# A recurrent attention and a two-layer FFN on one core: transposes by DMA of two chunks in one transfer, the first pair in halves by heads, and a new order of all steps

## The chip, the cores and the metric

The kernel runs on one core of one Trainium2 chip. A core has five engines with instruction streams of their own: TensorE (PE) multiplies matrices, VectorE (DVE), ScalarE (ACT) and GpSimd (POOL) work elementwise, and SyncE (SP) issues nearly all DMAs. The metric is the device time of one execution in microseconds (us); lower is better. Before the change three runs took 182.15, 182.19 and 182.31 us, median 182.19.

## The reference

Inputs `r`, `k`, `v`, `w` have the shape (4, 8, 768, 48): batch, heads, sequence, head dimension, in float32. For each batch and head a 48 x 48 state runs over the sequence, and the result goes through a feed-forward network (FFN) with a leaky relu:

```
for t in range(S):
    cur     = u * k_t  outer  v_t
    y_t     = r_t @ (state + cur)
    state   = w_t[:, None] * state + k_t outer v_t
x = y as (3072 tokens, 384)
out = max(0.01 h, h) @ w_out,   h = x @ w_in      # 384 -> 2048 -> 384
```

## The kernel before

**Chunks.** The sequence is cut into chunks of 128 positions, six for each of four batches, 24 in all. Inside a chunk the decays become a cumulative sum of logarithms, so that with r' = r exp(sum) and k' = k exp(-sum) the outputs are a masked product: scores = k' r'^T for all eight heads, times a triangular mask, times v, plus r' times the state that came in. The bonus with u is a term of its own (POOL products, a DVE reduction, a POOL product). Chunks 0 to 3 are done as two *pairs* (function `pair`: two chunks of one batch at once, with positions interleaved), and chunks 4 to 23 by `single`.

**Steps of a single chunk.** Four loads (L701, SP, 192 KB each) bring w, k, r, v into one "in" slot. ACT takes the logarithm (L711), PE the cumulative sum (L717, L720), DVE adds (L729), ACT makes the two exponentials (L743, L747), DVE the products r' and k' into an "rk" tile (L405). Then rk is transposed to rkT, either by PE (L416, evacuated by DVE L421 or ACT L423) or by one DMA transpose on SP's queue (L764): the set `RK_DMA` says which chunks go by DMA, 13 of them. PE makes the scores (L858), for one chunk or, where `MERGED` says so, for two chunks in one step. DVE masks them (L788), PE multiplies by v and by the state (L829, L824), DVE adds the bonus and writes y (L478). y is transposed into xT, by PE (L464) and a copy (L469, L471), or by a DMA transpose (L843) for the eight chunks in `Y_DMA`. The state goes on through L798 and L811 or L813, with POOL's L775.

**Steps of a pair.** One load brings both chunks of a tensor, 384 KB (L490). One logarithm (L502), three cumulative sums (L510), a total (L524), four exponentials of 384 columns (L543), four products (L405), four transposes by PE, scores in two steps (L624), four masks of 512 columns (L636), sums (L583), the state (L594, L601), intra (L649), inter (L656), bonus (L668), two copies to y (L678, L680), two transposes.

**FFN.** The list `blocks` groups the chunks into blocks of one or two. For each block an up step (L901) is six matmuls of 256 columns for a block of two, or twelve of 128 for a block of one, into one PSUM bank of 512 columns; ACT applies the leaky relu (L916); a down step (L928) is four matmuls of 384 columns. DVE or ACT copies a chunk's output (L939, L941) and SP stores it (L945). The FFN weights come in float32 and are cast to bf16 by ACT, DVE and POOL (L357 to L361), each into place from an "in" slot.

**What sets the order.** Nothing is scheduled on the chip: every engine runs its list from first to last, and waits where an input is not there. The class `Plan` makes the lists while the program is built. It holds steps with durations for each engine that could do them, priorities (chunk number times ten, the FFN from 1000 on), buffers from pools of fixed size, and a model of the DMA queue with a wire time for each kind of transfer. It steps through time and starts, on each free engine, the ready step of lowest priority number whose buffers are free. `RANK` shifts the priority of single steps, `FORCE` fixes the engine. Where the plan sees PE idle in the first 24 us, it adds filler matmuls on zeros (L970).

**Queues.** All loads, stores and transposes are on SP's one queue, in the order of the list, each issue waiting for its own buffers and for the transfer eight places before it.

Of the kernel before, what the change touches and what calls it, by code (L numbers as in the profile page):

```python
# [8 lines left out]
F32 = mybir.dt.float32  # L9
BF16 = mybir.dt.bfloat16  # L10
# [5 lines left out]
class Buf:  # L16


    def __init__(self, pool, kind=None):
        self.pool, self.kind, self.users, self.t, self.free_at = pool, kind or pool, [], None, 0.0  # L20


class Plan:
# [18 lines left out]
    def order(self, pools):  # L42
# [10 lines left out]
        remain = {k: len(b.users) for k, b in bufs.items()}  # L53
        free_tiles = {p: [(0.0, k) for k in range(len(t))] for p, t in pools.items()}
# [18 lines left out]
        while events:  # L73
# [13 lines left out]
            for e in self.ENGINES:  # L87
# [3 lines left out]
                while ready[e]:  # L91
                    pri, i = heapq.heappop(ready[e])
                    if self.start[i] is not None:
                        continue
                    want, ok = {}, True
                    for b in self.steps[i][5]:
                        if b.t is None:
                            want[b.pool] = want.get(b.pool, 0) + 1
                            if in_use.get(b.kind, 0) >= self.limits.get(b.kind, 99):
                                ok = False  # L100
                    for p, k in want.items():
                        if sum(f <= now + 1e-9 for f, _ in free_tiles[p]) < k:
                            ok = False
# [10 lines left out]
                for b in takes:  # L114
                    if b.t is None:
                        slots = free_tiles[b.pool]
                        s = min(slots)
                        slots.remove(s)
                        b.slot = s[1]
                        b.t = pools[b.pool][s[1]]  # L120
                        in_use[b.kind] = in_use.get(b.kind, 0) + 1
# [9 lines left out]
                else:  # L131
# [5 lines left out]
                    self.done[i] = dma_free + lat + (self.late if now > 20 else 0.0)  # L137
                heapq.heappush(events, (free[e], 1, e, -1))
# [5 lines left out]
                for b in {id(b): b for b in (*reads, *takes)}.values():  # L144
                    b.free_at = max(b.free_at, self.done[i])
                    remain[id(b)] -= sum(u == i for u in b.users)
                    if remain[id(b)] == 0:
                        free_tiles[b.pool].append((b.free_at, b.slot))
                        heapq.heappush(events, (b.free_at, 2, "*", b.kind))
# [6 lines left out]
BOTH = (1.5, 64, 1.45, 0.2)  # L156
WEIGHT = (2.08, 24, 2.6, 0.2)
# [4 lines left out]
RANK = {0: 15.37, 1: 14.4, 2: 3.33, 3: 23.03, 4: 38.76, 5: 12.01, 6: -26.8, 7: -21.87, 8: -21.96, 9: -19.05,  # L162
# [16 lines left out]
FORCE = {23: "DVE", 26: "DVE", 29: "ACT", 30: "DVE", 46: "ACT", 58: "ACT", 61: "ACT", 79: "ACT", 85: "DVE",  # L179
    112: "DVE", 114: "ACT", 117: "DVE", 119: "ACT", 121: "ACT", 123: "DVE", 125: "POOL", 127: "ACT", 128:  # L180
    "POOL", 134: "POOL", 137: "DVE", 139: "POOL", 142: "ACT", 143: "POOL"}
# [3 lines left out]
def kernel(  # L185
# [37 lines left out]
    blocks = [2, 1, 1, 1, 1, 2, 2, 2, 2, 2, 1, 1, 2, 2, 2]  # L223
# [17 lines left out]

    trev = pool.tile([128, 128], BF16, name="trev")
# [12 lines left out]
    xT = pool.tile([128, KT, NCH * L], BF16, name="xT")  # L255

    make("in", 10, [128, 1536], F32)
    make("lw", 3, [128, H, 64], BF16)
    make("lw2", 1, [128, 2, H, 64], BF16)
    make("ci", 2, [128, H, D], F32)  # L260
    make("rk", 5, [128, 2, H, 64], BF16)
    make("rkT", 4, [128, 2 * NP, 128], BF16)
    make("rkT2", 2, [128, 2 * NP, 256], BF16)
    make("vb", 6, [128, H, D], BF16)
    make("ru", 2, [128, H, D], F32)
    make("dg", 3, [128, H], F32)
    make("vs", 4, [128, H, D], F32)
    make("m", 3, [128, 2, NP, 128], BF16)
    make("a", 3, [128, NP, 2], F32)
    make("s", 6, [128, NP, 2, D], F32)  # L270
    make("sb", 4, [128, NP, 2, D], BF16)
    make("y", 4, [128, H, D], BF16)
    make("g", 3, [128, NJ, max(blocks) * L], BF16)
    make("o", 5, [128, DM], F32)
    make("ps", 8, [128, 512], F32, psum)

    with tc.manual_schedule():
# [41 lines left out]
        plan = Plan({"hp": 2, "op": 2, "cp": 1, "ek": 1, "yy": 2, "warm": 1, "warm2": 1}, SLACK_FROM, SLACK, LATE)  # L319
# [87 lines left out]
        def transposes(P0, rk, kind, s_d, rkTb, out_of, pri_k=0):  # L407
# [6 lines left out]
            def tpose(e):  # L414
                for g in range(NP):
# [3 lines left out]
            def evac(e):  # L419
                if e == "DVE":  # L420
                    nc.vector.tensor_copy(out=out_of(), in_=view()[:, 0:NP, :])  # L421
                else:
                    nc.scalar.copy(out=out_of(), in_=view()[:, 0:NP, :])  # L423

            s_tr = step({"PE": 0.23}, tpose, P0, deps=[s_d], reads=[rk], takes=[tr])
            return step({"DVE": 0.42, "ACT": 0.59}, evac, P0, deps=[s_tr], reads=[tr], takes=[rkTb])
# [48 lines left out]
        def add_bonus(P0, y, yp, vs, s_y, s_vs):  # L475
            return step(
                {"DVE": 0.55},
                lambda e: nc.vector.tensor_tensor(out=y.t[:], in0=heads(yp.t), in1=vs.t[:], op=ALU.add),  # L478
                P0 + 1, deps=[s_y, s_vs], reads=[yp, vs], takes=[y])
# [3 lines left out]
        def pair(n):  # L483
            P0 = n * 10
            b = seq[n][0]
            slots = [Buf("in"), Buf("in")]
            lds = {}
            for name, src, si, off in (("w", w, 0, 0), ("k", k, 0, 1), ("r", r, 1, 0), ("v", v, 1, 1)):
                def load(e, src=src, si=si, off=off):
                    nc.sync.dma_start(  # L490
                        out=slots[si].t[:, off * 768 : (off + 1) * 768].rearrange("p (h f) -> p h f", h=H),
                        in_=src[b, :, 0 : 2 * L, :].rearrange("h (p j) d -> p h (j d)", j=2))
                lds[name] = [step({"SP": 0.65}, load, P0 + len(lds) * 0.1, takes=[slots[si]], wire=BOTH)]

            def view(si, off, j):
                return lambda: slots[si].t[:, off * 768 : (off + 1) * 768].rearrange(
                    "p (h j d) -> p h j d", h=H, j=2)[:, :, j, :]

            lw = Buf("lw2")
            s_ln = lns[n] = step(  # L500
                {"ACT": 0.85},
                lambda e: nc.scalar.activation(  # L502
                    out=lw.t[:, :, :, 0:D].rearrange("p j h d -> p h j d"),
                    in_=slots[0].t[:, 0:768].rearrange("p (h j d) -> p h j d", h=H, j=2), func=AF.Ln),
                P0, deps=lds["w"], reads=[slots[0]], takes=[lw])

            def cum(bank, mats):
                def go(e):
                    for j in range(2):
                        nc.tensor.matmul(  # L510
                            heads(bank.t), lhsT=mats[j][:], rhs=lw.t[:, j, :, 0:D], start=(j == 0), stop=(j == 1),
                            skip_group_check=True)
                return step({"PE": 0.33 if n else 0.55}, go, P0, deps=[s_ln], reads=[lw], takes=[bank])

            c1, c0, cg, e0 = (Buf("ps", "cp2") for _ in range(4))
            s_c1 = cum(c1, (tstr2, tinc2))
            s_c0 = cum(c0, (tinc2, tinc2))
            s_cg = cum(cg, (tstr2, tstr2))
            firsts[n] = s_c1
# [485 lines left out]
```

## Time and profile before

| | |
|---|---|
| median of three runs | 182.19 us |
| the profiled execution | 181.38 us |
| its span, first to last instruction | 179.6 us |
| mean granted PE clock | 0.996 |
| PE busy | 171.6 us (96%) |
| DVE, ACT, POOL busy | 115.0, 115.3, 102.5 us |
| DMA moved | 34.43 MB in 116571 packets |
| first FFN matmul | 19.00 us |
| last score step of the attention | 156.84 us |
| matmuls end, last copy begins | 176.0 us |
| DMA transposes rkT: count, median to landing | 13, 3.9 us |
| DMA transposes xT: count, median to landing | 8, 3.7 us |

The page is a sum over one execution. "Busy" of PE counts each matmul from start to end, and matmuls overlap in the array, so 96% is not 96% of peak; what a matmul costs the stream is read from the distance of the starts in the timeline. Idle time stands behind a group with the work that ended it. The chain of waits is followed back from the last instruction.

### The profile page before, as it was taken

How to read it: one execution, taken by the hardware profiler on the slowest of the kernel's cores; microseconds unless marked ns; L12 is line 12 of the kernel's file. 1: busy time of each engine (PE TensorE's matmuls, PEld its weight loads, DVE VectorE, ACT ScalarE, POOL GpSimd, SP SyncE). 2: the span in 40 equal slices, each digit the busy share in tenths (PEclk: the TensorE clock that was granted, in tenths of full speed). 3: DMA queues.
4: the chain of work that ended last, by engine and by line, in shares of the span. 5: the costliest groups of instructions: out<-in, count | busy, mean ns of one | idle time of the engine just before them, and what ended most of it. 6: DMA issues, size and time to landing. Idle time of an engine off the chain costs nothing.

```text
span 179.6 us, 5197 instructions
## 1 busy us (share of the span) xinstructions
PE 171.6 (96%) x2036; PEld 129.8 (72%) x2037; DVE 115.0 (64%) x231; ACT 115.3 (64%) x253; POOL 102.5 (57%) x138
## 2 busy tenths in 40 slices
PE   7798999999999999999999999999999999999991
PEld 2466888867778788877788767787788786787850
DVE  7699764289789898559677558397468297241102
ACT  2678968855867788884489774485486664652610
POOL 5999632574897686877469854667165665100000
PEclk9999999999999999999999999999999999999998
DMA  5999999998999999999999989999899996600112
GB/s 141 261 283 316 370 376 364 187 199 199 231 191 224 180 229 134 184 213 173 185 181 223 212 179 223 153 215 175 152 254 170 220 163 134 167 9 19 47 44 88
DMA packets 116571, 34.43 MB, mean 192 GB/s; under 512 B 109121, under 2 KB 115778, under 8 KB 116546
## 3 DMA queue, kind: packets, MB, share of 16 engines
q1 hardware_dynamic: 116544, 34.09, 95.8%
q8 instruction: 16, 0.26, 0.7%
q14 instruction: 9, 0.07, 0.1%
q10 hardware_dynamic: 2, 0.00, 0.0%
HBM read 25.17 MB, written 4.72 MB: 166 GB/s over the span
## 4 chain that ended last, share of the span: by engine, by line
PE 77%; DMA 11%; DVE 4%; ACT 2%; issue 2%; SPq 1%; POOL 0%; DVEq 0%; ACTq 0%
PE ps L901 35%; PE ps L928 28%; DMA in<-in_r_dram 3%; DMA in<-in_v_dram 3%; DMA in<-in_w_dram 2%; PE ps L858 2%; DMA xT<-y 2%; PE ps L829 2%; PE ps L717 2%; PE ps L824 2%; PE ps L416 2%; DVE rk L405 2%; PE ps L798 1%; PE ps L464 1%; DVE m L636 1%
## 5 line engine op out<-in xcount | busy, mean ns | idle before, releaser
L901 PE MATMUL ps<-xT,w_in_b 128*128 128x256 bf16 (+1 forms) x720 | 73.3, 251 | 0.4 <-ACT xT L471 0.2
L928 PE MATMUL ps<-w_out_b,g 128*128 128x384 bf16 x384 | 73.4, 326 | 0.0
L916 ACT ACTIVATE g<-ps 128x512 bf16<-128x512 f32 x96 | 56.8, 597 | 25.4 <-PE ps L901 23.2
L901 PEld LDWEIGHTS <-w_in_b 128*128 128x128 bf16 x720 | 57.8, 98 | 9.9 <-issue 0.7
L928 PEld LDWEIGHTS <-g 128*128 128x128 bf16 x384 | 35.2, 98 | 17.3
L405 DVE TENSOR_TENSOR rk<-in,ps 128x384 bf16<-128x384 f32 x46 | 24.5, 548 | 9.9 <-ACT ps L743 6.5
L435 POOL TENSOR_TENSOR ru<-in,ub 128x384 f32<-128x384 f32 x24 | 23.9, 1001 | 9.6 <-DMA in<-in_k_dram 7.6
L788 DVE TENSOR_TENSOR m<-ps,maskb 128x512 bf16<-128x512 f32 x40 | 25.1, 683 | 5.3 <-PE ps L858 5.3
L439 POOL TENSOR_TENSOR ru<-ru,in 128x384 f32<-128x384 f32 x24 | 24.6, 1027 | 3.0 <-DMA in<-in_r_dram 2.4
L775 POOL TENSOR_TENSOR sb<-s,a 128x384 bf16<-128x384 f32 x18 | 15.0, 831 | 16.8 <-ACT a L738 16.8
L447 POOL TENSOR_TENSOR vs<-in,dg 128x384 f32<-128x384 f32 x20 | 16.6, 830 | 9.1 <-DVE dg L443 8.4
L729 DVE TENSOR_TENSOR ci<-ps,lw 128x384 f32<-128x384 f32 x20 | 11.1, 555 | 9.7 <-PE ps L720 4.5
L939 DVE COPY o<-ps 128x384 f32<-128x384 f32 x10 | 5.6, 555 | 15.6 <-PE ps L928 15.4
L443 DVE TENSOR_REDUCE dg<-ru 128x8 f32<-128x384 f32 x24 | 12.9, 544 | 2.1 <-POOL ru L439 2.1
L478 DVE TENSOR_TENSOR y<-ps,vs 128x384 bf16<-128x384 f32 x20 | 11.1, 553 | 3.2 <-PE ps L829 2.6
L455 POOL CAST vb<-in 128x384 bf16<-128x384 f32 x24 | 12.0, 504 | 1.5 <-DMA in<-in_v_dram 1.4
L711 ACT ACTIVATE lw<-in 128x384 bf16<-128x384 f32 x20 | 10.4, 522 | 2.9 <-DMA in<-in_w_dram 2.9
L743 ACT ACTIVATE ps<-ps 128x384 f32<-128x384 f32 x20 | 9.6, 481 | 4.1 <-DVE ci L729 3.6
L738 ACT ACTIVATE a<-ps 64x4 f32<-64x4 f32 x36 | 6.0, 167 | 7.7 <-DVE ci L729 5.1
L813 DVE TENSOR_TENSOR s<-ps,sb 128x384 f32<-128x384 f32 x14 | 7.7, 552 | 3.8 <-PE ps L798 2.7
L747 ACT ACTIVATE ps<-ci 128x384 f32<-128x384 f32 x20 | 9.8, 491 | 0.0
L941 ACT COPY o<-ps 128x384 f32<-128x384 f32 x14 | 6.7, 479 | 4.2 <-PE ps L928 4.0
(90 smaller groups left out, 176.2 us busy)
## 6 DMA issues: line engine op xcount, KB each, us to landing
out_dram<-o SPq DMA_DIRECT2D x24, 192.0 KB, 3.7
in<-in_w_dram SPq DMA_DIRECT2D x20, 192.0 KB, 4.2
in<-in_k_dram SPq DMA_DIRECT2D x20, 192.0 KB, 4.2
in<-in_r_dram SPq DMA_DIRECT2D x20, 192.0 KB, 4.0
in<-in_v_dram SPq DMA_DIRECT2D x20, 192.0 KB, 4.0
in<-in_moe_w_out_dram SPq DMA_DIRECT2D x4, 768.0 KB, 12.1
in<-in_moe_w_in_dram SPq DMA_DIRECT2D x4, 384.0 KB, 6.8
in<-in_moe_w_in_dram SPq DMA_DIRECT2D x2, 768.0 KB, 9.0
```

Source lines behind the costliest of these rows:

```text
L405: (nc.gpsimd if e == "POOL" else nc.vector).tensor_tensor(out=o, in0=x, in1=i, op=ALU.mult)
L435: lambda e: nc.gpsimd.tensor_tensor(out=ru.t[:], in0=kv(), in1=ubv, op=ALU.mult),
L439: lambda e: nc.gpsimd.tensor_tensor(out=ru.t[:], in0=ru.t[:], in1=rv(), op=ALU.mult),
L443: lambda e: nc.vector.tensor_reduce(out=dg.t[:], in_=ru.t[:], axis=AX.X, op=ALU.add),
L447: lambda e: nc.gpsimd.tensor_tensor(out=vs.t[:], in0=vv(), in1=dg.t[:].unsqueeze(2).to_broadcast([128, H, D]), op=ALU.mult),
L455: {"POOL": 0.56}, lambda e: nc.gpsimd.tensor_copy(out=vb.t[:], in_=vv()),
L478: lambda e: nc.vector.tensor_tensor(out=y.t[:], in0=heads(yp.t), in1=vs.t[:], op=ALU.add),
L775: lambda e: nc.gpsimd.tensor_tensor(out=sb.t[:].rearrange("p g a d -> p (g a) d"), in0=s_in.t[:].rearrange("p g a d -> p (g a) d"), in1=a_ ...
L788: lambda e, par=par: nc.vector.tensor_tensor(out=m.t[:, par, :, :], in0=sc[par].t[:].rearrange("p (g t) -> p g t", g=NP), in1=maskb[:].uns ...
L901: nc.tensor.matmul(hp.t[:, a * N : (a + 1) * N], lhsT=w_in_b[:, t, (j + a) * 128 : (j + a + 1) * 128], rhs=xT[:, t, c0 : c0 + N], start=(a ...
L916: lambda e, hp=hp, g=g, j=j, J=J, N=N: nc.scalar.activation(out=g.t[:, j : j + J, 0:N], in_=hp.t[:, 0 : J * N].rearrange("p (a n) -> p a n ...
L928: nc.tensor.matmul(op.t[:, 0:DM], lhsT=g.t[:, j, off : off + 128], rhs=w_out_b[:, j, :], start=(j == 0), stop=(j == NJ - 1))
```

## The change

1. **Merged transposes.** Where two chunks' scores are merged, their rk tiles are now two neighbouring slots of one tile, and one DMA transpose (128 x 2048 elements) fills two neighbouring rkT slots. It is issued after both chunks' r' and k'. In the same way a pair's two y tiles go in one transfer (128 x 768) into two neighbouring chunks of xT, whose layout becomes chunk by chunk. There are 6 merged and 1 single rk transpose (13 single before) and 4 merged and 2 single for y (8 single before). Chunks 22 and 23 become a merged pair.
2. **The first pair in halves.** For the pair at chunk 0, loads of w, k and r, the logarithm, the cumulative sums, exponentials, products, transposes, scores and masks are done for four heads at a time. In both pairs intra becomes two steps or four by parity and half, and the order of the products that are added into y is free.
3. **Buffers.** "in" 10 to 7, lw 3 to 2, rk stays 5 and rkT becomes 5 in place of 4 + 2 wide ones, vb 6 to 10, ru 2 to 3, vs 4 to 3, m 3 to 5, s 6 to 5, y 4 to 3, g 3 to 2, o 5 to 24. Limits on PSUM banks: up results ("hp") 2 to 4, cumulative sums and one exponential 1 to 2, attention outputs 2 to 4.
4. **The plan.** It also keeps PE from starting on a bank that another engine still uses; 0.4 us are added to every DMA after 20 us (0 before), the slack of 0.2 us a step goes; `RANK` has a number for nearly every step in place of 144, `FORCE` is new, and `blocks` has 14 entries, four of them of one chunk, in place of 15 with six.

By the lists, PE has 25 fillers in place of 40, 12 score steps for the singles in place of 13, and 42 transposes of y in place of 48; the 88 of rk stay. SP's list has the first store behind 38 loads of the singles, where it was behind nine. The copy of ub (L399) goes from DVE to ACT.

```diff
-    RK_DMA = {6, 11, 12, 14, 15, 16, 17, 18, 19, 20, 21, 22, 23}
-    Y_DMA = {8, 10, 16, 17, 20, 21, 22, 23}
-    MERGED = {6, 10, 12, 14, 16, 18, 20}
-    LEAD = 4
-    AHEAD = 4
-    SLACK_FROM = 50
-    SLACK = 0.2
-    LATE = 0.0
+    RK_DMA = {9, 12, 13, 14, 16, 17, 18, 19, 20, 22}
+    Y_DMA = {13, 14, 15, 17, 18, 19, 20, 22}
+    MERGED = {6, 10, 12, 14, 16, 18, 20, 22}
+    PARTS = {0: [(0, NP // 2), (NP // 2, NP)]}
+    HALVES = "wkr"
+    LIMITS = {"hp": 4, "op": 2, "cp": 2, "ek": 2, "yy": 4, "warm": 1, "warm2": 1}
+    LEAD = 6
+    AHEAD = 7
+    SLACK_FROM = 45
+    SLACK = 0.0
+    LATE = 0.4
...
-    blocks = [2, 1, 1, 1, 1, 2, 2, 2, 2, 2, 1, 1, 2, 2, 2]
+    blocks = [2, 2, 1, 1, 2, 1, 2, 2, 1, 2, 2, 2, 2, 2]
...
+    def make2(name, count, shape, dtype):
+        t = pool.tile([shape[0], count, *shape[1:]], dtype, name=name)
+        pools[name] = [t[:, i] for i in range(count)]
+        pools[name + " wide"] = [t[:, i : i + 2] for i in range(count - 1)]
...
-    xT = pool.tile([128, KT, NCH * L], BF16, name="xT")
+    xT = pool.tile([128, NCH, KT, L], BF16, name="xT")
...
+            parts = PARTS.get(n, [(0, NP)])
...
+                cuts = parts if name in HALVES else [(0, NP)]
+                for x, (g0, g1) in enumerate(cuts):
...
+            for x, (g0, g1) in enumerate(parts):
+                P = x, g0, g1
+                wide = (g1 - g0) / NP
+                s_k0 = exp(c1, e0, -1.0, [s_c1[x]], [c1], [e0], *P)
...
         def run(ns):
-            works = [single(n) for n in ns]
+            two, P1 = None, ns[-1] * 10
+            if len(ns) == 2:
+                rk2, rkT2 = (Buf("rk", wide=2), Buf("rkT", wide=2)) if ns[0] in RK_DMA else (None, None)
+                two = [rk2, rkT2, Buf("y", wide=2) if ns[0] in Y_DMA else None, [], [], []]
+            works = [single(n, two, x) for x, n in enumerate(ns)]
             asked = [next(x) for x in works]
+            if two and two[0]:
+                two[4].append(step(
+                    {"SP": 1.3},
+                    lambda e: nc.sync.dma_start_transpose(
+                        out=rkT2.t.rearrange("p x g t -> p (x g) t"), in_=rk2.t.rearrange("p x a h d -> p (x a h d)")),
+                    P1, deps=two[3], reads=[rk2], takes=[rkT2], wire=TRK2))
...
+            if two and two[2]:
+                s_x = step(
+                    {"SP": 1.3},
+                    lambda e: nc.sync.dma_start_transpose(
+                        out=xT[:, ns[0] : ns[0] + 2].rearrange("p x g t -> p (x g) t"),
+                        in_=two[2].t.rearrange("p x h d -> p (x h d)")),
+                    P1 + 1, deps=two[5], reads=[two[2]], wire=TY2)
```

More of the change, by code (lines that the diff above doesn't have):

```diff
@@ L113, in order @@
                 engs, fn, pri, deps, reads, takes, wire = self.steps[i]
[L114 to L121, printed above, removed]
+                for b, k in given:
+                    gone = range(k, k + b.wide)
+                    free_tiles[b.pool] = [x for x in free_tiles[b.pool] if x[1] not in gone]
+                    b.slot = k
+                    b.t = pools[b.pool if b.wide == 1 else b.pool + " wide"][k]
+                    in_use[b.kind] = in_use.get(b.kind, 0) + 1
                 d = engs[e]
@@ L137, in order @@
                     self.done[i] = dma_free + lat + (self.late if now > 20 else 0.0)
+                for b in (*reads, *takes):
+                    if e == "PE":
+                        b.written = max(b.written, self.done[i])
+                    else:
+                        b.other = max(b.other, self.done[i])
                 heapq.heappush(events, (free[e], 1, e, -1))
@@ L156 @@
 BOTH = (1.5, 64, 1.45, 0.2)
+PART = (0.75, 32, 1.45, 0.2)
 WEIGHT = (2.08, 24, 2.6, 0.2)
@@ L414, in tpose @@
             def tpose(e):
-                for g in range(NP):
+                for g in range(g0, g1):
                     nc.tensor.transpose(
@@ L497, in view, with some, cum @@
                     "p (h j d) -> p h j d", h=H, j=2)[:, :, j, :]
+            def some(name, g0, g1):
+                return [*{x: 0 for x in lds[name][g0:g1]}]
             lw = Buf("lw2")
[L500 to L507, printed above, removed]
+            s_lns = [step(
+                {"ACT": 0.16 + 0.69 * (g1 - g0) / NP},
+                lambda e, h0=2 * g0, h1=2 * g1: nc.scalar.activation(
+                    out=lw.t[:, :, h0:h1, 0:D].rearrange("p j h d -> p h j d"),
+                    in_=slots[0].t[:, 0:768].rearrange("p (h j d) -> p h j d", h=H, j=2)[:, h0:h1, :, :], func=AF.Ln),
+                P0 + 0.5 * x, deps=some("w", g0, g1), reads=[slots[0]], takes=[lw]) for x, (g0, g1) in enumerate(parts)]
+            lns[n] = s_lns[0]
+            def cum(bank, mats, x, g0, g1):
                 def go(e):
@@ new lines, in pair, with summed, intra @@
+            yps, begun = [Buf("ps", "y2"), Buf("ps", "y2")], set()
+            def summed(x, out, **k):
+                nc.tensor.matmul(out, start=x not in begun, stop=True, skip_group_check=True, **k)
+                begun.add(x)
+            s_yi = []
+            for i, (g0, g1) in enumerate(parts):
+                for par in range(2):
+                    def intra(e, g0=g0, g1=g1, par=par):
+                        for h in range(2 * g0 + par, 2 * g1, 2):
+                            for js in range(2):
+                                for x in range(2):
+                                    q = slice(64 * x, 64 * x + 64)
+                                    summed(x, yps[x].t[:, h * D : (h + 1) * D], lhsT=ms[js].t[q, par, h // 2, :],
+                                           rhs=vbs[js].t[q, h, :])
+                    s_yi.append(step(
+                        {"PE": 0.35 * (g1 - g0) / NP}, intra, P0 + 1, deps=[s_ms[i, 0, par], s_ms[i, 1, par], *s_vbs],
+                        reads=[*ms, *vbs], takes=yps))
@@ L664, in add_vs @@
+            s_y1 = step(
+                {"PE": 0.19}, inter, P0 + 1, deps=[s_sb, *(s for x in s_T for s in x)], reads=[rkTb, sb], takes=yps)
             def add_vs(e):
```

314 lines of the change are left out of this document (177 added, 137 removed), and 149 rows, old and new, of the table RANK.

## The prediction

> **What bounds the kernel now.** I read the page's busy shares and slices first, then the table by stage, then the chain that ended last, then the TensorE (PE) timeline around each pause.
>
> ```profile
> span 179.6 us, 5197 instructions
> ...
> PE 171.6 (96%) x2036; PEld 129.8 (72%) x2037; DVE 115.0 (64%) x231; ACT 115.3 (64%) x253; POOL 102.5 (57%) x138
> ...
> PEclk9999999999999999999999999999999999999998
> ...
> 0.00:19.00 19.00, 15.41 (x225) 9.35 (x227) 15.51 (x43) 12.32 (x26) 15.82 (x31) 1.00 1.05 257
> ...
> 25.70:156.80 131.10, 130.58 (x1558) 101.30 (x1557) 90.18 (x173) 90.38 (x207) 82.58 (x101) 1.00 1.09 199
> ```
>
> PE is busy 130.58 of 131.10 us between 25.7 and 156.8 us. From 25.7 us on, the end is set by how much PE still has to stream, plus its few pauses. Before 19 us it is not PE: VectorE (DVE) is busy 15.51 of 19, and many PE instructions are fillers. The chain says so too:
>
> ```profile
> 1.93 5.64 DMA in<-in_r_dram
> 7.67 0.99 DVE rk L405
> ...
> 11.32 0.27 DVE m L636
> ...
> 13.59 0.68 DVE m L636
> ...
> 18.22 0.74 ACT xT L471 x2
> 19.00 1.47 PE ps L901 x12
> ```
>
> The first pair waits for r (7.67), then runs through DVE to its last mask multiply (13.59 + 0.68 = 14.27), through ScalarE (ACT) to xT, and the first FFN matmul starts at 19.00. So three things count: the opening, PE's sum afterwards, PE's pauses afterwards. Two of the pauses, and one that is no wait:
>
> ```profile
> 47.86 0.36 PE L829 MATMUL ps<-vb,m 128*128 128x48 bf16 x8
> 48.45 0.32 PE L717 MATMUL ps<-lw,trev 128*128 128x384 bf16 x1 [0.23 <-ACT lw L711]
> ...
> 54.15 0.62 PE L858 MATMUL ps<-rkT 48*128 48x128 bf16 x16
> 54.70 0.51 PE L901 MATMUL ps<-xT,w_in_b 128*128 128x128 bf16 x6
> ...
> 61.05 0.82 PE L928 MATMUL ps<-w_out_b,g 128*128 128x384 bf16 x4
> 62.08 0.70 PE L901 MATMUL ps<-xT,w_in_b 128*128 128x256 bf16 x5 [0.20 <-ACT xT L471]
> ```
>
> Starts, not durations, give PE's price, because matmuls overlap. Eight of L829 stream in 0.20, but 0.59 passes: 0.38 lost, waiting for a w load. Four of L928 take 0.65, but 1.03 passes: 0.37 lost, waiting for an xT copy. With four smaller ones (52.9, 60.6, 88.3, 116.9: 0.19, 0.10, 0.14, 0.07) the real waits after 25.7 us are 1.25. At 54.15 sixteen score matmuls occupy 0.55 where pairs of them stream in about 0.45, and the instruction ahead of them is held 0.10 too: each score step costs about 0.2 beyond its columns.
>
> **The change, part by part.** Prices by starts: up step of 256 columns (6 matmuls) 0.655, matmul of 128 columns 0.056, of 384 columns 0.1625.
>
> *PE's sum.* Two more y chunks are transposed by DMA (before 8, after 10: singles 13 and 17, pairs from 14, 18, 20, 22): 6 x 0.056 = -0.33. Four one-chunk FFN blocks in place of six: 96 matmuls of 128 columns become 48 of 256: 5.38 - 5.23 = -0.14. One more merged pair, so 12 score steps for 13: -0.22. Sum -0.7. The rk transposes by PE stay 88, and 13 chunks of rk go by DMA as before (six pairs and one single).
>
> *The opening, in halves.* DVE's price per column follows from two rows:
>
> ```profile
> L405 DVE TENSOR_TENSOR rk<-in,ps 128x384 bf16<-128x384 f32 x46 | 24.5, 548 | 9.9 <-ACT ps L743 6.5 <-ACT ps L747 2.4 <-ACT ps L543 0.8
> L788 DVE TENSOR_TENSOR m<-ps,maskb 128x512 bf16<-128x512 f32 x40 | 25.1, 683 | 5.3 <-PE ps L858 5.3
> ```
>
> That is 0.145 fixed and 0.00105 a column, so a half rk costs 0.35 and a half mask 0.41. By the new order: the halves of w let Ln end at about 5.1 (before 5.42). The copy of ub now stands on ACT ahead of the exponentials, until 5.65. Half exponentials (0.31) follow, and DVE starts at 6.3 (before 6.51). DVE then has rk 6 x 0.35 + 2 x 0.47 (those that read ci from SBUF are dearer, 792 against 548), three evacuations 0.7, two reductions 1.09, eight half masks 3.3: 8.1, plus about 0.4 of waiting for exponentials. Last mask at 14.8, against 14.27, and the second pair's first rk (0.54) is not yet done, as it was before. From there: two rk and sb (1.65), the inter matmuls (0.4), then in ACT's order two y copies, an rkT evacuation, two xT copies, and the cast of w_in that the first up step needs (0.49 x 2 + 0.62 + 0.49 x 2 + 0.85): 14.8 + 1.65 + 0.4 + 3.4 = 20.3 for the first up, against 19.00. The new order has fewer holes behind it: by 25.9 us both have done all of both pairs, and the old one 36 up matmuls of 256 columns and some of the next block, the new one 30. Behind by 6 x 0.109 + 0.2 = 0.85. I take +0.9. Bounds: -0.5, if the halves pull the chain forward by the 0.7 us that half a load takes and ACT's order costs nothing; +1.6, if the DVE work meets POOL as the 0.98 us rk at 7.67 did.
>
> A step more of scores in the first pair also costs PE its 0.2; DVE's lateness covers that, and without the cover it is +0.2. [...]
>
> *Merged transposes.* They move the same blocks of 128 columns, so no DMA work is saved, but SP issues 13 transposes for 21. Their issues take 1.2 to 1.9 us of SP each; SP waits for others most of the time, so the gain is 0. Landing:
>
> ```profile
> DMA to landing us min/median/max: 3.0/3.9/5.7
> ...
> DMA to landing us min/median/max: 2.3/3.7/4.9
> ```
>
> The first line is rkT (8 blocks), the second xT (3 blocks). Five more blocks cost 0.7 at the minimum, 0.14 each: a merged rk transfer lands 1.1 later, a merged y 0.4 later. Bounds: 0, and a second whole landing (3.9, 3.7). Both chunks must now be ready before the issue, and loads queued on SP behind it wait too. What hides it is PE work between a chunk's last input and its use, summed from the new order. For rk, from the pair's last cumulative sum to the scores: 10.6 us for 16/17, 12.3 to 17 for the others. The chain needs 0.3 + 0.55 + 1.0 + 1.1 + 0.5, then 5.7 + 1.1: 10.2. For y, from intra to the first up: 8.4 for 14/15, 6.4 for 18/19, 5.2 for 20/21, 4.55 for 22/23. Need 0.75 + 4.9 + 0.4 = 6.1 while loads run, 0.75 + 2.3 + 0.4 = 3.5 at the end. So 0, with little to spare at 16/17 and 18/19.
>
> *Buffers and order.* Ten input slots become seven, two g buffers for three, 24 o buffers for five. The last weights are issued after casts that free their slots, so I see DMA idle for 1.2 to 1.7 us near 21 us. In exchange the stores move behind: the w load that was late at 47.9 us was the fifteenth transfer after the weights, and is the twelfth; a load of 192 KB at the 199 GB/s of the stage table takes 1.0 us. That wait goes. Next late: xT of one-chunk blocks, where 0.8 to 1.05 us of PE work covers about 0.8; 0.1 to 0.2 each. I take 0.55 of waits after 25.7 us. Bounds 0.3 and 3.0 (six score steps each waiting as long as the worst before, and the three tight y).
>
> Sum: 0.9 - 0.7 - 1.25 + 0.55 = -0.5. The profiled execution took 181.38 (span 179.6, 1.8 around it), so it would become 180.9. That execution lies 0.8 under the median of the runs, so the forecast is 182.19 - 0.5 = **181.7**.
>
> **The rivals.**
> - *The opening loses more* (slower). Halves add nine fixed parts of about 0.145 on DVE (four rk, four masks, one evacuation). Against: DVE idled 0.61 before r. With the opening at +2.0: 2.0 - 0.7 - 1.25 + 0.55 = +0.6, 182.8. It decides for slower from an opening 1.8 behind. Chance 0.18.
> - *The transposed pair comes late*. At 18/19, 20/21 and 16/17 PE stands until the transfer lands. For it: PE runs its list in order, and landing reached 5.7. From 1.5 times the single landing on it shows; at the bound of a second landing 18/19, 20/21 and 16/17 lose 1.8, 2.9 and 1.7, about +5.5. Middle +2, 184.2. Chance 0.16.
> - *The halves do shorten the opening*: -0.5 - 0.7 - 1.25 + 0.55 = -1.9, 180.3. For it: r's wait of 0.61 goes. Chance 0.22.
> - *The clock falls*. Fillers fall from 40 matmuls to 25. PE's first matmuls of 512 columns take 0.427, the one at 5.08 takes 0.226, and the clock stays 1.00 over pauses of 0.8. Opening work at half speed for a stretch of 3.4 us: +1.7, 183.4. Chance 0.02. [...]
>
> **How the numbers follow.** The forecast's case, 181.1 to 182.2, has 0.4: 0.26 of it faster, 0.14 within 0.2% (0.36 us, about what a measurement of this kernel can tell). Faster: 0.26 + 0.22 = 0.48. Same: 0.14 + 0.04 from the edges of the slow cases = 0.18. Slower: 0.14 + 0.15 + 0.02 + 0.03 unnamed = 0.34. The range runs from the third rival to the middle of the second, 180.3 to 184.2.
>
> **What would show it.** Right: last half mask near 14.8 us, first up near 20.3, PE without a hole from 26 us on, no score step waiting for rkT, 1.1 us more to landing for merged rk. Wrong: first up before 19; PE idle at up steps behind a merged y; DMA holes between 40 and 110 us with PE waiting for lw; a PE clock under 1.00 before 20 us.

## The result and the profile after

The changed kernel took 183.95 us (median of five, 183.89 to 185.60), the kernel before beside it 182.19 (five, 181.34 to 183.07). The ratio is 1.0123, 95% interval 1.0074 to 1.0172: slower by 1.2%, where 0.3% faster was forecast. The ratios here and below are worked out from the fast runs of both kernels (those at most 1.5% above the fastest of the same kernel; here with a sixth run of 184.83), and not from the two medians, which alone would give 1.010. The time lies inside the forecast's range of 180.3 to 184.2, but on the other side of the kernel before. The profiled execution of the changed kernel is its slowest (185.6), that of the kernel before nearly its fastest (181.38). So these two profiles differ by 4.2 us where the medians differ by 1.8, and more profiles of either follow below.

From the page of the changed kernel, the span, the busy times and the clock's row; then its table by stage (columns as before: time, then busy time of PE, PE's loads, DVE, ACT, POOL, then clock, DMA share, GB/s):

```profile
span 183.7 us, 5052 instructions
...
PE 175.3 (95%) x1974; PEld 129.6 (71%) x1974; DVE 118.1 (64%) x243; ACT 115.3 (63%) x259; POOL 98.8 (54%) x134
...
PEclk9999999999999999999999999999999999999999
```

```profile
0.00:19.00 19.00, 16.16 (x163) 8.72 (x163) 14.07 (x44) 10.22 (x27) 15.46 (x31) 1.00 1.02 256
19.00:25.70 6.70, 6.46 (x131) 4.65 (x131) 6.42 (x12) 6.11 (x13) 2.27 (x4) 1.00 0.54 143
25.70:156.80 131.10, 130.06 (x1485) 99.53 (x1483) 92.83 (x181) 88.00 (x202) 81.03 (x100) 1.00 1.04 205
```

PE has 163 instructions in the first 19 us where it had 225, and is busier with them (16.16 against 15.41). They take longer. Why is in the chain of waits of the changed kernel, in order of time, from the first pair's scores (L823) to the second pair's first exponential (L733):

```profile
11.80 0.85 PE ps L823 x15
12.65 0.33 PE ps L1197 x2
12.98 0.36 PE ps L823 x7
13.34 1.93 PE ps L1197 x5
15.27 0.65 PE ps L697 x2
15.92 0.02 issue
15.94 0.50 ACT ci L733
```

L1197 are the fillers, and they lie on the path. Five of them stand ahead of the cumulative sums of the second pair (L697), which had their input since ACT's logarithm ended at 12.61. Behind that logarithm ACT sat idle for 3.34 us. The timeline of PE, first of the changed kernel, then of the kernel before at the same work (L970 fillers, L510 sums):

```profile
5.50 0.69 PE L697 MATMUL ps<-lw,tstr 128*128 128x192 bf16 x3
...
13.27 2.00 PE L1197 MATMUL ps<-zeros 128*128 128x512 bf16 x5
15.06 0.85 PE L697 MATMUL ps<-lw,tinc 128*128 128x384 bf16 x2
...
16.27 0.49 PE L697 MATMUL ps<-lw,tstr 128*128 128x384 bf16 x2
```

```profile
5.48 0.48 PE L510 MATMUL ps<-lw,tstr 128*128 128x384 bf16 x2
...
11.43 0.50 PE L970 MATMUL ps<-zeros 128*128 128x512 bf16 x3
11.77 0.33 PE L510 MATMUL ps<-lw,tstr 128*128 128x384 bf16 x1
```

Start to start, 384 columns take 0.16 us in the kernel before from 5.5 us on, and 0.32 in the changed one until 16.2 us (fillers of 512: 0.427). PE runs at half rate there, though the clock's row says 9 in every slice. The first FFN matmul comes at 22.30, against 19.00.

From here on an execution is split in two numbers. *Left* is the PE work that starts after 26.0 us, each matmul at the price of a streaming row (128 columns 0.055 us, 256 0.109, 384 0.162, score matmuls in pairs). *Lost* is the distance of starts after 26 us beyond that, pauses of score steps included. 26 + left + lost is 5.7 us short of the time in every execution below.

| execution | full rate from | first FFN | left | lost | time |
|---|---|---|---|---|---|
| before, shown ahead | 4.1 | 19.00 | 145.28 | 4.45 | 181.38 |
| before, second | 4.9 | 18.98 | 145.22 | 6.75 | 183.66 |
| before, third | 3.9 | 19.09 | 145.28 | 5.19 | 182.16 |
| changed, first | 16.2 | 22.30 | 147.69 | 6.22 | 185.60 |
| changed, second | 16.2 | 22.23 | 147.58 | 5.36 | 184.68 |
| changed, third | 15.4 | 21.27 | 146.65 | 5.40 | 183.77 |

On average the changed kernel has 2.05 us more left at 26 us and loses 0.2 more after it. The loss is the opening's.

### The profile page after: what moved, and what is told of

Read it like the earlier page. It is cut to its first block, busy times and chain, and to the rows that moved or that the text cites. A ratio compares the mean times of both kernels' runs of the same rounds, so it can differ in the third digit from the quotient of the medians.

```text
span 183.7 us, 5052 instructions
## 1 busy us (share of the span) xinstructions
PE 175.3 (95%) x1974; PEld 129.6 (71%) x1974; DVE 118.1 (64%) x243; ACT 115.3 (63%) x259; POOL 98.8 (54%) x134
## 4 chain that ended last, share of the span: by engine, by line
PE 56%; DMA 15%; SPq 9%; ACT 6%; DVE 6%; issue 4%; POOL 2%; DVEq 0%; POOLq 0%; ACTq 0%
PE ps L1128 23%; PE ps L1155 19%; SPq L903 9%; DMA in<-in_w_dram 5%; DMA in<-in_r_dram 4%; DMA in<-in_v_dram 4%; PE ps L1197 3%; DVE rk L579 2%; DMA xT<-y 2%; ACT g L1143 2%; PE ps L1076 2%; PE ps L1036 1%; PE ps L1031 1%; PE ps L919 1%; PE ps L823 1%
## 5 line engine op out<-in xcount | busy, mean ns | idle before, releaser
L1155 PE MATMUL ps<-w_out_b,g 128*128 128x384 bf16 x384 | 70.8, 326 | 0.1
L1128 PE MATMUL ps<-xT,w_in_b 128*128 128x256 bf16 (+1 forms) x672 | 69.4, 258 | 0.7 <-DMA xT<-y 0.7
L1143 ACT ACTIVATE g<-ps 128x512 bf16<-128x512 f32 x96 | 54.5, 605 | 20.3 <-PE ps L1128 16.4
L1128 PEld LDWEIGHTS <-w_in_b 128*128 128x128 bf16 x672 | 57.1, 98 | 9.0 <-DMA xT<-y 1.1
L579 DVE TENSOR_TENSOR rk<-in,ps 128x384 bf16<-128x384 f32 (+1 forms) x49 | 25.1, 525 | 11.3 <-DMA in<-in_r_dram 4.1
L1168 ACT COPY o<-ps 128x384 f32<-128x384 f32 x13 | 6.2, 478 | 15.5 <-PE ps L1155 15.4
L590 PE MATMUL ps<-ident,rk 128*128 128x128 bf16 x88 | 9.4, 235 | 1.8 <-DVE rk L579 1.7
L1166 DVE COPY o<-ps 128x384 f32<-128x384 f32 x11 | 6.1, 554 | 5.1 <-PE ps L1155 5.0
```

Source lines behind the costliest of these rows:

```text
L579: (nc.gpsimd if e == "POOL" else nc.vector).tensor_tensor(out=o, in0=x, in1=i, op=ALU.mult)
L1128: nc.tensor.matmul(hp.t[:, a * N : (a + 1) * N].rearrange("p (s n) -> p s n", n=L), lhsT=w_in_b[:, t, (j + a) * 128 : (j + a + 1) * 128], ...
L1143: lambda e, hp=hp, g=g, j=j, J=J, N=N: nc.scalar.activation(out=g.t[:, j : j + J, 0:N], in_=hp.t[:, 0 : J * N].rearrange("p (a n) -> p a n ...
L1155: nc.tensor.matmul(op.t[:, 0:DM], lhsT=g.t[:, j, off : off + 128], rhs=w_out_b[:, j, :], start=(j == 0), stop=(j == NJ - 1))
```

## The experiments

**Repeats (a_rep, b_rep): both kernels unchanged.**

> The changed kernel once more. In its first profile TensorE's matmuls of 512 columns took 0.427 us until about 16 us, those of the kernel before 0.226 from 4.1 us on. Theory A, the half rate belongs to that one execution (185.6 us, the slowest of five): an execution near 183.9 shows 0.22 from 4 to 8 us on and the first FFN matmul at 20.5 to 21.3 us in place of 22.3. Theory B, the half rate belongs to the changed opening: again 0.427 until 13 us or later, first FFN matmul at 22 or later, whatever the time. By both the median is 183.9 to 184.5, and the pauses after 26 us come to about 1.8 us more than before.

> The kernel before once more. Theory A (half rate by chance of the execution): an execution near 183 shows matmuls of 512 columns at 0.427 us beyond 4.1 us, one near 181.4 does not. Theory B: 0.226 from 4.1 us on in every execution, and the first FFN matmul at 18.8 to 19.2 us.

Measured: 184.73 (six, 183.85 to 184.96), ratio 1.0113 [1.0071, 1.0155], and one execution of 183.66 of the kernel before; the table has their profiles. The changed opening is again at half rate to 16.2 us: theory A falls. The kernel before at 183.66 has the same opening as at 181.38. It lost 2.3 us more after 26 us, for an xT that came late:

```profile
129.00 0.66 PE L901 MATMUL ps<-xT,w_in_b 128*128 128x128 bf16 x9 [1.02 <-DMA xT<-y]
```

**Halves joined (a_whole)**, with the order kept. Part 0 covers all heads, part 1 emits nothing; so for loads, logarithms, sums, exponentials, products, scores, masks and intra, here for the sums:

```diff
+            def joined(fn, g0, g1):
+                if g0:
+                    return lambda e: None
+                return lambda e: fn(e, 0, NP)
...
-                    {"PE": (0.33 if n else 0.55) * (g1 - g0) / NP}, go, P0 + 0.5 * x, deps=[s_lns[x]], reads=[lw], takes=[bank])
+                    {"PE": (0.33 if n else 0.55) * (g1 - g0) / NP}, joined(go, g0, g1), P0 + 0.5 * x, deps=[s_lns[x]], reads=[lw], takes=[bank])
```

> The changed kernel in its own order, with the two halves of each step of the first pair joined into one instruction at the place of the first half; nothing else differs. Theory C, the halves cost the opening: DVE saves nine fixed parts of 0.145, 1.3 us, the first FFN matmul comes 0.8 to 1.3 us sooner and the time falls to 182.6 to 183.2. Theory D, the opening is late for what stands around the halves (copy of ub on ACT, order behind the masks, late weights): 183.6 to 184.3. If the halves help as the third rival had it, 184.3 to 185.3.

Measured: ratio 1.0105 [1.0045, 1.0166], single times from 183.78 to 187.99. Half rate to 16.8 us, first FFN matmul at 22.40. Joined halves gain nothing here, but the half rate may hide what they do; see a_warm_whole.

**Merged transposes as singles, each behind its chunk (a_split):**

```diff
+            def made(o, i, v):
+                mult(o, i, v)
+                left[0] -= 1
+                if left[0] == 0 and rkb.wide == 2:
+                    nc.sync.dma_start_transpose(out=rkT.t, in_=rk.t.rearrange("p a h d -> p (a h d)"))
...
+                           yb.wide == 2 and nc.sync.dma_start_transpose(
+                               out=xT[:, n], in_=y.t.rearrange("p h d -> p (h d)"))),
```

> The changed kernel with every merged transpose given back as two single ones, each issued right behind the last write of its own chunk. Theory E, the merged transfers are late for their uses: the pause of 0.85 us behind the merged y at 156.6 us goes, and the time falls by 0.5 to 1.0, to 182.9 to 183.4. Theory F, the merged transfers cost nothing: 183.7 to 184.2; the ten more issues of 1.2 to 1.9 us on SP could make it slower still, to 185.

Measured: 191.1. This run tells nothing of its question. A single transpose of rk was issued before the rkT slot's last reader in the order, so that the scores of another chunk read the new contents; what it computes is changed there, and PE waits in other places. a_singles below puts it right.

**Five more fillers (a_warm)**, behind the eighth, ninth and eleventh step of PE:

```diff
+            if plan.eng[i] == "PE" and plan.steps[i][0]["PE"] > 0:
+                pe_count += 1
+                for n in {8: (512, 128), 9: (256,), 11: (512, 128)}.get(pe_count, ()):
+                    nc.tensor.matmul(warm.t[:, 0:n], lhsT=zeros[:, 0:128], rhs=zeros[:, 0:n], start=True, stop=True,
+                                     skip_group_check=True)
```

> The changed kernel with five more filler matmuls (1536 columns) between the transposes of 7.2 to 9.6 us, where TensorE stood idle; nothing else differs. Theory G, the half rate of TensorE until 16 us makes the opening late (two executions of the changed kernel: 0.427 us for 512 columns until 16.0 us, fillers and sums of the second pair 1.0 to 1.5 us late behind it): the full rate is there by 9 to 11.5 us, the second pair's cumulative sums start by 13.7 in place of 15.0, the first FFN matmul comes at 20.8 to 21.3 in place of 22.2, the time falls to 182.9 to 183.6. Theory D, the order of DVE and ACT sets the opening and the rate only follows: first FFN matmul at 22.0 to 22.4, 184.0 to 184.7.

Measured: 182.96 (twelve, 181.53 to 184.35) beside 182.55; ratio 1.0017 [0.9988, 1.0047], where the changed kernel has 1.0123 and 1.0113. Five fillers take away nearly all of the loss. Timeline of PE of this kernel (L1206 and L1198 are fillers):

```profile
7.33 0.74 PE L1206 MATMUL ps<-zeros 128*128 128x512 bf16 x2
...
8.92 0.49 PE L1206 MATMUL ps<-zeros 128*128 128x512 bf16 x2
...
13.05 0.87 PE L1198 MATMUL ps<-zeros 128*128 128x512 bf16 x4 [0.16 <-issue]
13.76 0.49 PE L697 MATMUL ps<-lw,tinc 128*128 128x384 bf16 x2
```

The rate is full from 9.0 us on, the fillers ahead of the sums take 0.87 for 2.00, and the sums start 1.3 sooner. The scores of the second pair start at 19.00, where the changed kernel's second profile has them at 21.00. (In this one execution, the slowest of the twelve, PE then stood 2.0 us for nothing that the profile shows, so its first FFN matmul is at 21.93.)

**More input slots (a_slots)**, given out in turn over the same order:

```diff
-    make("in", 7, [128, 1536], F32)
+    make("in", 10, [128, 1536], F32)
...
-    make("o", 24, [128, DM], F32)
+    make("o", 12, [128, DM], F32)
```

> The changed kernel in its own order, with ten input slots in place of seven and twelve output buffers in place of 24, given out in turn. Theory H, seven slots hold the last weights back (SP stands from 15.7 to 22.9 us, DMA moves 147 GB/s from 19 to 26 us) and so the first loads after them (sum of chunk 4 waits 0.38 us at 38.2, DVE for r at 52): DMA moves over 300 GB/s there, the pause at 38.2 and one or two of those at 52 to 79 us go, 183.6 to 184.1 at most 0.4 to 1.0 below the changed kernel. If the late weights do not matter: 184.3 to 184.9.

Measured: 184.74, ratio 1.0126 [1.0084, 1.0169]. Its stage table shows the hole in the DMA filled (363 GB/s for 143):

```profile
19.00:25.70 6.70, 6.30 (x130) 4.66 (x129) 6.42 (x12) 6.11 (x14) 2.54 (x5) 1.00 1.05 363
```

The pause at 38.2 us is gone too, and the time is that of the changed kernel (ratios 1.0104 to 1.0123). The seven slots cost no time that shows.

**Merged transposes as singles, once more (a_singles)**: rk in the place of the merged one, y as in a_split:

```diff
-                    lambda e: nc.sync.dma_start_transpose(
-                        out=rkT2.t.rearrange("p x g t -> p (x g) t"), in_=rk2.t.rearrange("p x a h d -> p (x a h d)")),
+                    lambda e: [nc.sync.dma_start_transpose(
+                        out=rkT2.t[:, x], in_=rk2.t[:, x].rearrange("p a h d -> p (a h d)")) for x in range(2)],
```

> The changed kernel with each merged transpose given back as two single ones: of y, each behind its own chunk; of rk, both at the place of the merged one. Theory E, a merged y is late for its up step: the pause at 156.6 us (0.85 in one execution, none in the next) is in no execution, 0.2 to 0.6 less. Theory F, merged transfers cost nothing: 184.2 to 185.0, ten more issues of SP included.

Measured: ratio 1.0136 [1.0077, 1.0196], single times 183.64 to 189.65. The interval takes in the changed kernel's ratios, so singles bring nothing. Timeline of PE, in its one profile, an execution of 187.79 us:

```profile
159.16 2.78 PE L1128 MATMUL ps<-xT,w_in_b 128*128 128x256 bf16 x24 [1.31 <-DMA xT<-y]
163.47 0.40 PE L1078 MATMUL ps<-rkT 48*128 48x128 bf16 x8 [0.55 <-DMA rkT<-rk]
```

In the changed kernel merged rkT lands in 4.3/4.8/6.0 us (minimum, median, maximum) and merged xT in 2.9/3.5/4.4. Theory E expected the pause near 157 us in no execution; here it is there with singles too, and the time doesn't fall.

**The kernel before without its eight first fillers (b_cold):**

```diff
-                if s < WARM_UNTIL and plan.steps[i][0]["PE"] > 0:
+                if pe_free > 1.1 and s < WARM_UNTIL and plan.steps[i][0]["PE"] > 0:
```

> The kernel before without the eight fillers ahead of its first matmul, all later ones kept. This makes its opening slow in the way that is suspected of the changed kernel. Theory G: 512 columns take 0.427 us until past 10 us, the first FFN matmul comes 0.8 to 1.8 us later than 19.0, and the time rises to 183.0 to 184.0. If the rate of the opening does not matter: first FFN matmul at 18.9 to 19.3, 182.0 to 182.5.

Measured: ratio 1.0038 [1.0005, 1.0071]. The miss is in the rate: with the later fillers still there, the profiled execution had the full rate from 8.7 us on, and its first FFN matmul came at 19.27.

**Fillers ahead of the sums (a_nf, a_warm_nf), and the halves again (a_warm_whole).** a_nf leaves out the fillers ahead of step 21 of PE, the second pair's first sum; a_warm_nf is a_warm with that too; a_warm_whole is a_whole with a_warm's fillers.

```diff
-                if s < WARM_UNTIL and plan.steps[i][0]["PE"] > 0:
+                if s < WARM_UNTIL and plan.steps[i][0]["PE"] > 0 and pe_count != 20:
```

> The changed kernel without the four or five fillers that stand ahead of the second pair's cumulative sums (13.3 to 15.0 us); the clock is left as it is. Theory G, second form: at half rate those fillers take 1.6 to 2.0 us in place of 0.9 and hold the sums up: sums at 13.2 to 13.6 in place of 15.0, still at half rate, first FFN matmul at 20.9 to 21.7 in place of 22.2, 183.6 to 184.3 against 184.7. If the rest of the opening is the bound (DVE's masks until 15.5): 184.4 to 185.0.

> The changed kernel with the five early fillers of 7.2 to 9.6 us, and without those ahead of the second pair's sums. Early fillers alone gave 182.96 (12 runs) beside 182.55 of the kernel before. If the late fillers still cost something at full rate: sums at 12.7 to 13.0 in place of 13.8, 0.3 to 0.7 us less, 182.2 to 182.7. If DVE's masks, done near 15, are the bound by then: 182.7 to 183.2.

> The changed kernel with the early fillers, and the halves of the first pair joined. Here the rate is full from 9 to 10 us on, so that the halves can be judged. Theory C, halves cost: last mask 0.5 to 1.0 sooner than with halves, 182.0 to 182.6. Third rival, halves help: last mask and first FFN matmul 0.3 to 0.8 later, 183.3 to 184.0. Neither: 182.7 to 183.2.

Measured: a_nf 183.33, ratio 1.0040 [1.0002, 1.0077]; a_warm_nf 182.93, 0.9997 [0.9968, 1.0027]; a_warm_whole 183.69, 1.0056 [1.0025, 1.0087]. So about 0.7% of the changed kernel's 1.1% goes when the fillers ahead of the sums are left out. And halves joined come out slower than halves (1.0056 against 1.0017 for a_warm), but the intervals overlap: that the halves help, by some 0.7 us, is likely and not shown. Theory C falls, and the third rival was probably right in sign.

Timeline of PE of a_nf:

```profile
12.15 0.80 PE L697 MATMUL ps<-lw,tinc 128*128 128x384 bf16 x2 [0.67 <-ACT lw L688]
12.74 0.53 PE L697 MATMUL ps<-lw,tstr 128*128 128x384 bf16 x1
...
19.74 0.83 PE L1128 MATMUL ps<-xT,w_in_b 128*128 128x256 bf16 x6
```

The logarithm ended at 12.10, so the sums start 0.05 us behind it, where the changed kernel's start 2.45 us behind it. They run at half rate here too: the first two take 0.59 us from start to start.

The profiles of a_nf and a_warm_nf caught executions at full rate from 4.8 us on, with the same PE instructions up to 7.2 us as those at half rate. There the first FFN matmul comes at 19.74 and 19.75 and 145.13 and 145.35 us are left, as in the kernel before. They also show the rate fall back to half. Table by stage of a_nf, in steps of 1 us, the clock third from the end:

```profile
11.00:12.00 1.00, 0.48 (x9) 0.29 (x9) 0.95 (x4) 0.74 (x1) 1.00 (x3) 0.79 1.22 258
12.00:13.00 1.00, 0.85 (x3) 0.41 (x3) 1.00 (x5) 0.11 (x2) 1.00 (x2) 0.50 1.27 275
13.00:14.00 1.00, 1.00 (x4) 0.30 (x2) 1.00 (x5) 0.80 (x2) 0.62 (x2) 0.50 1.08 336
14.00:15.00 1.00, 1.00 (x15) 0.51 (x16) 0.98 (x3) 0.82 (x3) 0.74 (x1) 0.50 1.03 372
15.00:16.00 1.00, 1.00 (x52) 0.96 (x46) 0.39 (x1) 0.31 (x2) 1.00 (x2) 1.00 1.13 306
```

In this execution, with no filler near 12 us, the clock is 0.50 from 11.6 to 15.0 us.

**Three steps moved (a_moves)**, on a_warm_nf:

```diff
         order = plan.order(pools)
+        for i, j in ((318, 311), (394, 395), (426, 448)):
+            order.remove(i)
+            order.insert(order.index(j) + 1, i)
```

> As the run with early fillers and without the late ones, and three steps moved by one to three places in the order: a reduction of the bonus behind two products, a product ahead of two state sums, a logarithm ahead of two small exponentials. Theory J, what is left of the loss after 26 us are steps of DVE and ACT placed in an order that makes TensorE wait at 65, 76 and 78 us, in every execution of the changed kernel alike (0.41, 0.22 and 0.55): these pauses fall under 0.1 each, 0.8 to 1.1 us less than without the moves. If the pauses come from late loads: no change from that run.

Measured: 182.42 (twelve, 181.03 to 183.77) beside 182.62, ratio 0.9956 [0.9918, 0.9995]. The pauses it aims at are in every profile of the changed kernel's order; here in the first:

```profile
66.41 0.40 PE L590 MATMUL ps<-ident,rk 128*128 128x128 bf16 x4 [0.25 <-DVE rk L579]
...
79.63 0.32 PE L919 MATMUL ps<-lw,trev 128*128 128x384 bf16 x1 [0.39 <-ACT lw L913]
```

With the moves these are gone, one of 0.27 behind g has come at 77.9, and a small one at 69.8 has grown. By starts 1.33 us of pauses at 65, 69, 76 and 79 us (0.41, 0.15, 0.22, 0.55) became 0.76 (0.32 and 0.44).

**The reverse, on the kernel before (b_few), and a_moves with one filler ahead of the sums (a_best):**

```diff
-                if s < WARM_UNTIL and plan.steps[i][0]["PE"] > 0:
+                if (pe_free == 1.1 or 14 < s < WARM_UNTIL) and plan.steps[i][0]["PE"] > 0:
```

```diff
-                if s < WARM_UNTIL and plan.steps[i][0]["PE"] > 0 and pe_count != 20:
+                if s < WARM_UNTIL and plan.steps[i][0]["PE"] > 0:
...
                     gap = s - pe_free - 0.1
+                    if pe_count == 20:
+                        gap = min(gap, 0.23)
```

> The kernel before with its eight first fillers, and without those between 4.3 and 14 us by its plan; nothing else differs. Theory G, third form: the fillers of the opening hold the rate up, and where they are thin the rate is half in most executions or falls back to half: 384 columns take 0.32 us somewhere between 7 and 14 us, the first FFN matmul comes 0.3 to 1.0 later than 19.0, the time rises by 0.4 to 1.3 to 182.9 to 183.9. Theory K, the phase of the clock alone decides: first FFN matmul at 18.9 to 19.2 in an execution that is at full rate by 5 us, no change of the median beyond 0.3.

> As the run with three moves (182.42, ratio 0.9956), with one filler of 512 columns ahead of the second pair's sums, where there was none, so that the rate does not fall back there. Theory G: sums at full rate in every execution, 0.2 to 0.5 less than with three moves, 181.9 to 182.3, and a ratio to the kernel before of 0.992 to 0.997. If the fall back does not matter: 182.3 to 182.7.

Both kernels a third time (a_rep2, b_rep2):

> The changed kernel a third time. Theory G: the profile is at half rate until past 9 us with the first FFN matmul at 22.2 or, with a chance of about a third, at full rate from 4.8 us on and then 20 to 21; the times fall in two groups, near 183.9 and 184.5 to 185.6. If it is at full rate from 4.8 us on and still at 22.2, the half rate is not the cause.

> The kernel before a third time. Theory G: full rate by 4 to 5 us or, where not, by 12 us, because its fillers go on; first FFN matmul at 18.9 to 19.6. Theory K: as in the changed kernel it can stay at half rate until 16 us, first FFN matmul past 20.

Measured: b_few 182.50 beside 182.46, ratio 1.0002 [0.9971, 1.0034]. Its profile has what theory G says of the opening: half rate until 14.1 us, the first FFN matmul at 20.26, 146.37 left:

```profile
12.42 1.17 PE L510 MATMUL ps<-lw,tinc 128*128 128x384 bf16 x3
13.38 0.85 PE L510 MATMUL ps<-lw,tstr 128*128 128x384 bf16 x2
```

but it loses only 4.39 after 26 us, and the median does not move. So half rate alone does not explain the changed kernel. Half rate *with five fillers ahead of the sums* is what the runs point to: a_nf leaves these fillers out, a_warm raises the rate, and each takes away most of the loss. That a_nf's gain is the fillers' alone is not shown: its one profile was at full rate from 4.8 to 11.6 us, and the rate in its other executions is not known. a_best: 182.58, 0.9991 [0.9963, 1.0020], no better than a_moves. Its one filler did not hold the rate: in its profile the clock is 0.50 from 11.7 to 15.1 us all the same. a_rep2: 184.92, 1.0104 [1.0061, 1.0146]; b_rep2: 182.16. The times of a_rep2 fall in two groups as expected (183.66 and 183.77, then 184.78 to 185.64), but the profile, of 183.77, was at half rate until 15.4 us, so the rate alone does not make the groups. That a_moves beats the kernel before (0.4%) hangs on one interval that ends at 0.9995, with a_best beside it at 0.9991; I take it as equal or a little faster.

## Why the prediction was wrong, step by step

**PE's sum, -0.7: right.** Streaming work of the whole program is 158.65 us by the prices above, 159.07 before: -0.42, for the -0.47 of y and blocks. One score step less is another 0.22.

**The opening, +0.9 with bounds of -0.5 and +1.6: the step that failed.** In the three executions 26 us found the changed kernel 2.4, 2.3 and 1.4 us behind in work left, which is 1.8 to 2.8 behind after its smaller sum. Three of its terms:
- The fillers were priced at nothing. The prediction counted that they fall from 40 to 25 and did not look where they stand. The kernel sizes them with full rate from 7.9 us of its plan on (`per = 0.00044`), five stand ahead of the second pair's sums, and at half rate they take 2.00 us (a_warm, at full rate: 0.87). The sums start at 15.06; in the kernel before at 11.77, behind three fillers of 0.34.
- PE's own steps were priced at full rate. Three rows of 384 columns stood in the trace of before at 0.16, and nothing said that this was a property of that opening.
- The product that reads ci from SBUF was put at 0.47 in halves. It took 1.21 and 0.62, and 1.40 for the second pair in the first profile, 0.56 in the third. That is most of what the third execution is better by. Why it varies stays open.

The last half mask ended at 15.55 for 14.8 and the first FFN matmul came at 22.3 for 20.3. With the rate full from 4.8 us (a_nf, a_warm_nf) it came at 19.75 and 145.1 to 145.4 were left, 0.3 to 0.5 behind after the smaller sum: by the work on DVE and ACT alone, the term was even too large.

**The rival with the clock, chance 0.02 and 183.4: this is the nearest to what happened**, near in time (183.95) and wrong in its reason: the rate did not fall, it came late. It was set low because the clock's row was 1.00 over pauses of 0.8. That row reads 1.00 from the start of both kernels, while the first fillers of 512 columns take 0.427 in both: the trace's record of the clock has its first entry at 4.1 us in the kernel before and at 16.2 in the changed one, and says nothing of the rate ahead of it. The distance of starts, which the prediction had used everywhere else, was the right witness. Its stretch of 3.4 us at half speed had no measurement under it: in the one profile ahead of the forecast, work runs at half from 1.26 to 4.1 us. The runs showed half until 15.4 to 16.2 us in the changed kernel and, after a full rate, for 3.4 us in a_nf (11.6 to 15.0) and a_best (11.7 to 15.1).

**Waits, 1.25 before and 0.55 after: both wrong.** The 1.25 came from one execution; the next two lost 2.3 and 0.7 us more. The second did not have the w wait at 47.9 us (0.38 in the first) and lost more at 52.7, 106 and 127.7 us; the third had that wait with 0.77 and one of 0.33 at 53.3 us. The 0.55 left out what the order of DVE and ACT does between 50 and 80 us: pauses of 0.20 to 0.33, 0.41, 0.15, 0.22 and 0.55 in every profile of the changed order (the last four gone or moved in a_moves and a_best). On average after 26 us 5.66 is lost against 5.46, so the expected -0.7 came as +0.2.

**Merged transposes, 0: right on the whole**, with landing up by 0.9 for rkT (1.1 said) and none for xT (0.4 said). A merged y near 154 to 158 us was late in five of the eleven profiles with merged transposes, by 0.3 to 1.5 us, and in time in six: the cover of 5.2 us that the prediction called tight is tight. Singles did not help (1.31 there in their one profile).

**Hole in the DMA near 21 us: right in place.** Its price, 0.38 at 38.2 us, could not be found in the time (a_slots).

**The third rival, halves help: probably right in sign**, some 0.7 us by a_warm_whole against a_warm, whose intervals overlap, and covered by the rest.

In sum: forecast -0.5, of it +0.2 by 26 us and -0.7 after. Measured +2.0 by the three ratios; by the table +2.05 is there at 26 us, and +0.2 comes after. With the rate and the fillers mended (a_warm_nf) the change is worth nothing, with three moves more at most -0.8. (The chances of the prediction add to 1.01, a slip that changes nothing.)

What stays open: how much is the half rate and how much the fillers it doubles. The ci product may play into it too: the second pair's took 0.55 us in a_nf's profile and 1.40 in the first two of the changed kernel. In the kernel before, with few fillers ahead of its sums, half rate cost 1.1 us at 26 us in the one profile and nothing in the median; I have no run that shows where that was made up.

## What to carry to other kernels

Where a program fills PE's idle time with matmuls on zeros, read from the starts whether they run at the rate they were sized for, and treat those ahead of a critical matmul as work on the path: sized for full rate, they held it up for about twice as long at half here (2.00 us, 0.87 in a_warm). Price waits from several executions; of the kernel before, the fastest profile showed the least of them (4.45 us lost, then 5.19 and 6.75). A row that says 1.00 where nothing was recorded is no evidence.

## What the runs showed of the hardware

The full rate began between 3.9 and 4.9 us in six profiles (the three of the kernel before, a_nf, a_warm_nf, a_best). It began at 8.7 us in b_cold and 9.0 in a_warm, with fillers near 5 to 10 us, and as late as 14.1 (b_few) to 16.8 us (a_whole) in others, with few or none there. Executions with the same PE instructions up to 7.2 us fall into both groups: a_nf had the full rate from 4.8 us on, the changed kernel's first profile from 16.2. In the latter PE streamed from 1.26 to 7.15 us with no pause over 0.15, and was at half rate all the same. In a_nf the rate went back to 0.50 from 11.6 to 15.0 us, and PE had been busy for 0.45 to 1.00 of each microsecond from 8 to 12. Why executions of the same instructions differ in the rate is not shown by these runs.
